# First MLP of a three-stage kernel: the next expert's first matrix is converted ahead of the ReLU, and the second MLP's weights are loaded two slots ahead

## The chip, the cores and the metric

The kernel runs on one core of one Trainium2 chip. The metric is the time of one execution on the device in microseconds (us), the median of several runs. Below, PE is TensorE, ACT is ScalarE, DVE is VectorE, POOL is GpSimd and SP is SyncE, which here only issues DMAs.

## The reference

A recurrent attention, then a mixture of eight experts with one expert for each token, then a plain gated MLP on all 3072 tokens. All in float32:

```python
def _moe_ref(x, modality_id, w_gate, modality_bias, w1, w2):   # x: (3072, 320), 8 experts, F = 1024
    logits = x @ w_gate + modality_bias[modality_id]
    e_idx = np.argmax(logits, axis=1)
    ...
    for e in range(E):
        mask = e_idx == e
        h = np.maximum(x[mask] @ w1[e], 0.0)
        out[mask] = gate_w[mask, None] * (h @ w2[e])

def _moe2_ref(x, w_in, w_out):                                  # w_in: (320, 2048), w_out: (2048, 320)
    h = x @ w_in
    g = h * (1.0 / (1.0 + np.exp(-1.702 * h)))
    return g @ w_out

def reference(**kwargs):
    ...
    return _moe2_ref(x=_moe_ref(x=attention, **moe), **moe2)
```

## The kernel before

Three stages follow each other on PE: the attention with the routing, the first MLP (the experts) and the second MLP. The change is in the first MLP, `moe1`, whose instructions stand in each engine's queue in the order in which they are written (`manual_schedule(engines=None)`): each engine takes its own queue strictly in that order, and semaphores hold an instruction until its operands are there.

Tokens are sorted by expert into slots of 128 rows. Slots 0 to 2 are done before this stage; `moe1` does slots 3 to 25 (`PLAN` is 3, `FIRST` is 4, `NFIX` is 26). Every float32 operand is carried as two float16 halves, high and low.

- `up` is a slot's 64 up products on PE: eight groups of eight, each into a quarter of a PSUM bank, five with the high half of the expert's first matrix and three with its low half. Then come the ReLU's halves: `hh` on ACT, twice 128x512, and `hl` = the rest on DVE, twice.
- `down` is the slot's 24 down products with the second matrix; ACT scales the sum into `ys`, POOL copies a token number into it, and SP stores it.
- `renew(i, n)` stands in an `If` on whether slot i has another expert than slot i-1. Where it has, `split(n)` converts the float32 matrix that lies ready in `raw1` or `raw2` into halves (ACT the high ones, DVE the low ones; eight pieces of 128x384 for the first matrix, five of 128x512 for the second), and POOL fetches the matrix that follows. All engines pass the branch, taken or not, and PE's low-half products wait until DVE has passed it. In this input the expert changes at slots 12, 14 and 25.
- `turn` transposes a slot's rows: on PE for slots 4 and 5, by a DMA transpose issued on SP three slots ahead for the others.
- `fill` is `step` of `weights2`. The second MLP's weights come as float64 in 22 parts of 512 KB (`s`). A step first writes the halves of the part before (ACT `WH` or `OH`, then DVE `WL` or `OL`), then issues the next part's load on SP, then makes float32 of its own part with five DVE instructions (`words`).
- `backs` and `flags` are small DVE work, once, after slot 8's `down`; `ready2` prepares the second MLP's first block in slots 16 to 23.
- `last` is the place for the second matrix of slot 25. It lies on the first matrix' halves, so it is written after slot 25's up products.

One iteration i of the loop is in this order: load of slot i+4's rows, `turn(i+3)`, `up(i+1)` with its ReLU halves, `renew(i+2, 1)`, `down(i)`, `renew(i+1, 2)`, `fill`. On PE up products of one slot and down products of the slot before alternate.

Of the kernel before, what the change touches and what calls it, by code (L numbers as in the profile page):

```python
# [484 lines left out]
F16 = mybir.dt.float16  # L485
# [22 lines left out]
PLAN = 3  # L508
# [3 lines left out]
class Mlp:  # L512
# [378 lines left out]
            out=xg.bitcast(I32), out_offset=None, in_=self.XD,  # L891
            in_offset=bass.IndirectOffsetOnAxis(ap=self.xrow[:, i:i + 1], axis=0))

    def up(self, xT, p, ps, mid=None, **k):

        nc = self.nc
        hh = p.tile([128, 8, 128], F16, tag="hh", name="hh")
        hl = p.tile([128, 8, 128], F16, tag="hl", name="hl")
        W = lambda t, k, f: t[:, f * 384 + k * 128:f * 384 + (k + 1) * 128]
        hi, lo = self.hi1, self.lo1  # L900
        for q in range(2):
            h = ps.tile([128, 4, 128], F32, tag="h", name="h", **k)
            for f4 in range(4):
                f = 4 * q + f4
                mms = [(W(hi, 0, f), xT[:, 0, :]), (W(hi, 1, f), xT[:, 1, :]), (W(hi, 0, f), xT[:, 2, :]),
                       (W(hi, 1, f), xT[:, 3, :]), (W(hi, 2, f), xT[:, 4, :]), (W(lo, 0, f), xT[:, 0, :]),
                       (W(lo, 1, f), xT[:, 1, :]), (W(lo, 2, f), xT[:, 4, :])]
                for j, (a, b) in enumerate(mms):
                    nc.tensor.matmul(h[:, f4, :], lhsT=a, rhs=b, start=(j == 0), stop=(j == 7))  # L909
            if mid and q == 0:  # L910
                mid()
            s = slice(4 * q, 4 * q + 4)
            nc.scalar.activation(hh[:, s, :], h, AF.Relu)  # L913
            nc.vector.scalar_tensor_tensor(hl[:, s, :], h, 0.0, hh[:, s, :], op0=ALU.max, op1=ALU.subtract)
        return hh, hl
# [35 lines left out]
    def moe1(self, fill, flags):  # L951
# [3 lines left out]
        with tc.tile_pool(name="m1", bufs=2, side="right", reuse_waits="tile") as p, \  # L955
# [16 lines left out]
            def turn(i):  # L972
                t = p.tile([128, 5, 128], F16, tag="xT", name="xT", bufs=3)
                x = xs[i].bitcast(F16)[:, 0:640]
                if i >= FIRST + 2:
                    nc.sync.dma_start_transpose(out=t, in_=x)
                else:
                    b = bank().bitcast(F16)[:, 0:640].rearrange("p (a b) -> p a b", a=5)
                    for j in range(5):
                        nc.tensor.transpose(b[:, j, :], x[:, 128 * j:128 * (j + 1)], self.id16)  # L980
                    nc.scalar.copy(t, b)
                xs[i] = xs[i], t
# [1 line left out]
            def bank():  # L984
                return ps.tile([128, 512], F32, tag="t", name="t")

            def up(i, mid=None):
                hs[i] = self.up(xs[i][1], p, ps, mid, bufs=4)

            def down(i, **k):  # L990
                self.down(i, xs.pop(i)[0], *hs.pop(i), p, ps, **k)

            last = self.hi1[:, 0:NW2], self.lo1[:, 0:NW2]
            xs[PLAN] = self.x0[PLAN], self.xT3
            for i in range(FIRST, FIRST + 3):
                load(i)
            load(FIRST + 3)
            self.fetch(1, self.wrow[:, FIRST:FIRST + 1])
            up(PLAN, lambda: turn(FIRST))
            self.fetch(2, self.wrow[:, FIRST:FIRST + 1])  # L1000
            for i in range(PLAN, NFIX - 1):
                if FIRST + 3 < i + 4 < NFIX:
                    load(i + 4)
                if i + 3 < NFIX:
                    turn(i + 3)
                up(i + 1, (lambda: turn(i + 2)) if i == PLAN else None)
                if i + 2 < FIRST + 2:
                    pass
                elif i + 2 < NFIX:
                    renew(i + 2, 1)  # L1010
                else:
                    with tc.If(new[i + 1] > 0):
                        self.split(2, last)
                    with tc.If(new[i + 1] < 1):  # L1014
                        nc.vector.tensor_copy(last[0], self.hi2)
                        nc.vector.tensor_copy(last[1], self.lo2)
                down(i)
                if FIRST + 2 <= i + 1 < NFIX - 1:
                    renew(i + 1, 2)
                fill(i)  # L1020
                if NFIX - 10 <= i <= NFIX - 3:
                    self.ready2(0, i - NFIX + 10, bank)
                if i == 8:
                    self.backs(bank()[:, 0:NE])
                    flags()
                if i == 14:
                    self.gather2(0)
                    nc.scalar.activation(self.between, self.between, AF.Sigmoid)
            down(NFIX - 1, to=last)
            fill(NFIX - 1)  # L1030

    def slots(self, fit, p, ps):

# [51 lines left out]
    def weights2(self, w_in, w_out, ctx):  # L1085
# [6 lines left out]
        n = 512  # L1092

        def load(src):
            s = q.tile([128, n], mybir.dt.uint64, tag="s", name="s")
            nc.sync.dma_start(out=s, in_=src)
            return s

# [16 lines left out]

        parts = [(w_in[:, k, a:a + n], lambda f, k=k, a=a: up(f, k, a)) for a in range(0, FF2, n) for k in range(3)]
        parts += [(flat(w_out)[:, n * i:n * i + n], lambda f, i=i: down(f, i)) for i in range(10)]
        staged, singles = [load(parts[0][0])], []

        def step():  # L1120

            if singles:
                f, work = singles.pop()
                work(f)
            if parts:
                work = parts.pop(0)[1]
                if parts:
                    staged.append(load(parts[0][0]))
                singles.append((single(staged.pop(0)), work))

        return step

    def before2(self, ctx):

# [787 lines left out]
def body(tc, A, out):  # L1922
    nc = tc.nc
    with ExitStack() as ctx:
# [8 lines left out]
        with ExitStack() as c1:  # L1933
# [53 lines left out]
            m.tab = ctx.enter_context(tc.tile_pool(name="tab", bufs=1, reuse_waits="tile"))  # L1987
            m.next(pool("m1x", 5))
            step = m.weights2(A["wi"], A["wo"], ctx)
            m.moe1(lambda i: step(), lambda: at.good(nc, m))  # L1990
        m.moe2(out)

        rv = nc.values_load(m.usual[0:1, 0:1], min_val=0, max_val=1)
# [36 lines left out]
```

## Time and profile before

| | |
|---|---|
| median of 3 runs | 1097.01 us (1094.71 to 1107.36) |
| the profiled execution | 1101.7 us, span of its instructions 1099.9 us |
| mean granted clock of TensorE | 0.883 of full speed |
| busy over the span | PE 914.2 us (83%), DVE 856.9 us (78%), ACT 676.5 us (62%), POOL 140.5 us (13%) |
| first MLP on PE | 563.6 to 760.2 us of the span |

The busy shares are means over three stages. For the first MLP the times from 563.6 to 760.2 us are to be read: what PE does there, how long it waits, and for whom. Times in the rows are microseconds from the start of the span.

### The profile page before, as it was taken

How to read it: one execution, taken by the hardware profiler on the slowest of the kernel's cores; microseconds unless marked ns; L12 is line 12 of the kernel's file. 1: busy time of each engine (PE TensorE's matmuls, PEld its weight loads, DVE VectorE, ACT ScalarE, POOL GpSimd, SP SyncE). 2: the span in 40 equal slices, each digit the busy share in tenths (PEclk: the TensorE clock that was granted, in tenths of full speed). 3: DMA queues.
4: the chain of work that ended last, by engine and by line, in shares of the span. 5: the costliest groups of instructions: out<-in, count | busy, mean ns of one | idle time of the engine just before them, and what ended most of it. 6: DMA issues, size and time to landing. Idle time of an engine off the chain costs nothing. (4 is left out here: it accounts for less than half of the span.)

```text
span 1099.9 us, 36916 instructions
## 1 busy us (share of the span) xinstructions
PE 914.2 (83%) x15548; PEld 672.5 (61%) x15548; DVE 856.9 (78%) x2094; ACT 676.5 (62%) x1476; POOL 140.5 (13%) x222
## 2 busy tenths in 40 slices
PE   0167886878798887889797888898999999999995
PEld 0155675666676666667686777784555555555553
DVE  8998999999999899988763887687666666666652
ACT  4477998998899899877632254243443434343432
POOL 2000000020020020011431223202012121111100
PEclk9999778987666786678799889998999999999998
DMA  3569779689869689695578668674011121121101
GB/s 112 128 151 182 142 157 176 115 179 187 174 159 179 135 169 185 106 133 91 186 145 148 147 184 237 156 150 126 7 31 42 31 43 34 41 35 43 37 1 27
DMA packets 249881, 129.53 MB, mean 118 GB/s; under 512 B 233248, under 2 KB 237088, under 8 KB 248544
## 3 DMA queue, kind: packets, MB, share of 16 engines
q1 hardware_dynamic: 243792, 98.34, 48.3%
q0 software_dynamic: 5808, 28.58, 8.5%
q8 instruction: 124, 2.03, 0.8%
q14 instruction: 61, 0.50, 0.1%
q10 hardware_dynamic: 96, 0.08, 0.0%
HBM read 57.78 MB, written 12.16 MB: 64 GB/s over the span
## 5 line engine op out<-in xcount | busy, mean ns | idle before, releaser
L1232 ACT ACTIVATE sg<-t 128x512 f32<-128x512 f32 x96 | 60.5, 630 | 183.7 <-DVE t L1230 183.7
L1226 PE MATMUL h<-xT,WH 128*128 128x512 f16 x480 | 119.3, 379 | 1.8 <-DVE g L1236 1.8
L1250 PE MATMUL acc<-OH,gh 128*128 128x320 f16 x384 | 114.8, 299 | 1.0 <-ACT gh L1238 1.0
L1250 PE MATMUL acc<-OH,gl 128*128 128x320 f16 x384 | 114.8, 299 | 0.6 <-DVE gl L1242 0.6
L1250 PE MATMUL acc<-OL,gh 128*128 128x320 f16 x384 | 114.8, 299 | 0.0
L909 PE MATMUL h<-xT,split 128*128 128x128 f16 x1408 | 91.9, 229 | 20.2 <-DVEq L964 11.5
L909 PEld LDWEIGHTS <-split 128*128 128x128 f16 x1472 | 91.7, 103 | 23.7 <-DVEq L964 12.9
L1230 DVE TENSOR_TENSOR t<-h,sB 128x512 f32<-128x512 f32 x96 | 66.2, 690 | 46.3 <-PE h L1226 46.3
L1250 PEld LDWEIGHTS <-gh 128*128 128x128 f16 x768 | 74.8, 98 | 44.3 <-ACT gh L1238 1.6
L1242 DVE TENSOR_TENSOR gl<-g,gh 128x512 f16<-128x512 f32 x96 | 66.3, 691 | 43.6 <-ACT gh L1238 43.6
L250 POOL DMA_INDIRECT XD<-XR,desti x24 | 31.1, 1295 | 468.0 <-ACT ust L250 314.9
L925 PE MATMUL y<-split,hh 128*128 128x320 f16 x368 | 81.2, 306 | 5.2 <-DVEq L1014 4.7
L1226 PE MATMUL h<-xT,WL 128*128 128x512 f16 x288 | 77.8, 379 | 0.0
L1226 PEld LDWEIGHTS <-WH 128*128 128x128 f16 x480 | 46.6, 98 | 44.8 <-DVE g L1236 3.4
L250 PE MATMUL w<-s,pick 128*128 128x160 f16 x368 | 65.5, 295 | 6.4 <-DVE s L250 2.3
L250 PEld LDWEIGHTS <-kb 64*128 64x128 f16 x2208 | 48.1, 101 | 35.6 <-issue 22.5
L1236 DVE SCALAR_TENSOR_TENSOR g<-h,sg 128x512 f32<-128x512 f32 x96 | 65.3, 680 | 0.0
L250 PEld LDWEIGHTS <-tbd 128*128 128x128 f16 x1152 | 51.2, 104 | 22.7 <-issue 9.9
L913 ACT ACTIVATE hh<-h 128x512 f16<-128x512 f32 x46 | 27.1, 594 | 54.2 <-PE h L909 54.1
L1238 ACT CAST gh<-g 128x512 f16<-128x512 f32 x96 | 59.3, 618 | 1.4 <-DVE g L1236 1.4
L925 PE MATMUL y<-split,hl 128*128 128x320 f16 x184 | 56.2, 306 | 0.0
L1264 POOL DMA_INDIRECT out<-o,ti x20 | 22.0, 1102 | 227.2 <-ACT o L1256 224.4
(357 smaller groups left out, 2403.4 us busy)
## 6 DMA issues: line engine op xcount, KB each, us to landing
K<-in_KVR SPq DMA_DIRECT2D x24, 480.0 KB, 4.9
raw<-in_AB SPq DMA_DIRECT2D x13, 640.0 KB, 4.0
s<-in_wi SPq DMA_DIRECT2D x12, 512.0 KB, 8.7
s<-in_wo SPq DMA_DIRECT2D x10, 512.0 KB, 4.8
raw<-in_WU SPq DMA_DIRECT2D x6, 660.0 KB, 4.2
YS<-ys SPq DMA_DIRECT2D x23, 160.5 KB, 6.4
Sd<-s SPq DMA_TRANSPOSE x46, 3.5
out<-o SPq DMA_DIRECT2D x14, 40.0 KB, 3.2
```

Of the source, the lines that this page charges most:

```text
L250: r = self.made[i] = getattr(getattr(self.nc, e), op)(*a, **k)
L909: nc.tensor.matmul(h[:, f4, :], lhsT=a, rhs=b, start=(j == 0), stop=(j == 7))
L913: nc.scalar.activation(hh[:, s, :], h, AF.Relu)
L925: nc.tensor.matmul(y, lhsT=a[:, f, :], rhs=V(b, f), start=(n == 0), stop=(n == 23))
L1226: nc.tensor.matmul(h3, lhsT=a, rhs=r, start=(j == 0), stop=(j == 7))
L1230: nc.vector.tensor_tensor(t, hs[k], self.xs[steps[k][0]]["sB"], op=ALU.mult)
L1232: nc.scalar.activation(sgs[k], t, AF.Sigmoid, scale=1.702)
L1236: nc.vector.scalar_tensor_tensor(gs[k], hs.pop(k), 2.0 ** -4, sgs.pop(k), op0=ALU.mult, op1=ALU.mult)
L1238: nc.scalar.copy(ghs[k], gs[k])
L1242: nc.vector.tensor_tensor(gls[k], gs.pop(k), ghs[k], op=ALU.subtract)
L1250: nc.tensor.matmul(accs[c], lhsT=a[:, s], rhs=r[:, f, :], start=(f == 0 and j == 0), stop=(f == NF - 1 and j == 2))
L1264: sent.append(nc.gpsimd.indirect_dma_start(out=out, out_offset=bass.IndirectOffsetOnAxis(ap=X["ti"][:, c:c + 1], axis=0), in_=o, in_offset ...
```

## The change

`up` is parted into `products` (PE alone) and `relu` (the halves), and `step` into `convert` (the halves of the part before) and `gather` (load and `words`). An iteration is now: `turn(i+3)`, the up products of slot i+1, `convert`, `renew(i+2, 1)`, the ReLU halves of slot i+1, `down(i)`, `renew(i+1, 2)`, `gather`. Two parts of `s` are loaded before the loop, and each `gather` loads the part two further on, into three buffers. `turn` is on PE for slots 4 to 7. `last` is a tile of its own, and slot 25's second matrix is converted into it ahead of slot 25's up products. `flags` comes two slots later.

```diff
-    def up(self, xT, p, ps, mid=None, **k):
-
-        nc = self.nc
-        hh = p.tile([128, 8, 128], F16, tag="hh", name="hh")
-        hl = p.tile([128, 8, 128], F16, tag="hl", name="hl")
+    def up(self, xT, p, ps):
+        return self.relu(self.products(xT, ps), p)
+
+    def products(self, xT, ps, mid=None, **k):
+
+        nc = self.nc
+        hs = []
...
+            hs.append(h)
             if mid and q == 0:
                 mid()
+        return hs
+
+    def relu(self, hs, p):
+
+        nc = self.nc
+        hh = p.tile([128, 8, 128], F16, tag="hh", name="hh")
+        hl = p.tile([128, 8, 128], F16, tag="hl", name="hl")
+        for q, h in enumerate(hs):
             s = slice(4 * q, 4 * q + 4)
             nc.scalar.activation(hh[:, s, :], h, AF.Relu)
...
-                if i >= FIRST + 2:
+                if i >= FIRST + 4:
                     nc.sync.dma_start_transpose(out=t, in_=x)
...
-            last = self.hi1[:, 0:NW2], self.lo1[:, 0:NW2]
+            last = p.tile([128, 2, NW2], F16, tag="last", name="last", bufs=1)
+            last = last[:, 0], last[:, 1]
...
-                if i + 3 < NFIX:
+                if FIRST + 4 <= i + 3 < NFIX:
                     turn(i + 3)
-                up(i + 1, (lambda: turn(i + 2)) if i == PLAN else None)
-                if i + 2 < FIRST + 2:
-                    pass
-                elif i + 2 < NFIX:
-                    renew(i + 2, 1)
-                else:
+                if i + 2 == NFIX:
                     with tc.If(new[i + 1] > 0):
                         self.split(2, last)
                     with tc.If(new[i + 1] < 1):
                         nc.vector.tensor_copy(last[0], self.hi2)
                         nc.vector.tensor_copy(last[1], self.lo2)
+                h = up(i + 1)
+                fill[0]()
+                if FIRST + 2 <= i + 2 < NFIX:
+                    renew(i + 2, 1)
+                hs[i + 1] = self.relu(h, p)
                 down(i)
                 if FIRST + 2 <= i + 1 < NFIX - 1:
                     renew(i + 1, 2)
-                fill(i)
+                fill[1]()
...
                 if i == 8:
                     self.backs(bank()[:, 0:NE])
+                if i == 10:
                     flags()
...
-            s = q.tile([128, n], mybir.dt.uint64, tag="s", name="s")
+            s = q.tile([128, n], mybir.dt.uint64, tag="s", name="s", bufs=3)
...
-        staged, singles = [load(parts[0][0])], []
+        staged, singles = [load(parts[i][0]) for i in range(2)], []
...
-                if parts:
-                    staged.append(load(parts[0][0]))
+                if len(parts) > 1:
+                    staged.append(load(parts[1][0]))
```

One iteration in DVE's queue, before. `split_152` is the first matrix, `split_153` the second, the `wt` row is the first of the five of `words`; rows marked BRANCH are the `If`:

```order
L914 SCALAR_TENSOR_TENSOR hl<-h,hh 128x512 x2
L963 TENSOR_LOAD chg
L964 COMPARE_AND_BRANCH
L886 SCALAR_TENSOR_TENSOR split_152<-raw_150,split_152 128x384 x8
L964 UNCONDITIONAL_BRANCH x2
L964 COMPARE_AND_BRANCH
L886 SCALAR_TENSOR_TENSOR split_153<-raw_151,split_153 128x512 x5
L964 UNCONDITIONAL_BRANCH x2
L1106 SCALAR_TENSOR_TENSOR WL<-f,WH 128x512
L1079 TENSOR_SCALAR wt<-s 128x512
```

The same iteration in DVE's queue, now:

```order
L1120 SCALAR_TENSOR_TENSOR WL<-f,WH 128x512
L974 TENSOR_LOAD chg
L975 COMPARE_AND_BRANCH
L886 SCALAR_TENSOR_TENSOR split_152<-raw_150,split_152 128x384 x8
L975 UNCONDITIONAL_BRANCH x2
L925 SCALAR_TENSOR_TENSOR hl<-h,hh 128x512 x2
L975 COMPARE_AND_BRANCH
L886 SCALAR_TENSOR_TENSOR split_153<-raw_151,split_153 128x512 x5
L975 UNCONDITIONAL_BRANCH x2
L1093 TENSOR_SCALAR wt<-s 128x512
```

The first matrix and its branch now stand ahead of `hl`, and `words` directly behind the second matrix; the next row behind the five of `words` is `WL` of the same part, where before it was `hl`.

SP's queue at the start of the stage, before (`xT` rows are DMA transposes, of slots 6 and 7):

```order
L1096 DMA s<-in_wi 128x512
L250 DMA YS<-xg_154 128x321
L976 DMA_TRANSPOSE xT<-xg 128x5x128
L934 DMA YS<-ys 128x321
L1096 DMA s<-in_wi 128x512
L976 DMA_TRANSPOSE xT<-xg 128x5x128
```

SP's queue at the start of the stage, now:

```order
L1110 DMA s<-in_wi 128x512 x2
L250 DMA YS<-xg_154 128x321
L945 DMA YS<-ys 128x321
L1110 DMA s<-in_wi 128x512
L974 TENSOR_LOAD chg
L974 ISA x2
L975 COMPARE_AND_BRANCH
L975 UNCONDITIONAL_BRANCH x2
L945 DMA YS<-ys 128x321
L1110 DMA s<-in_wi 128x512
L987 DMA_TRANSPOSE xT<-xg 128x5x128
```

Two parts are asked for at once, and the first DMA transpose, now slot 8's, comes behind the fourth part.

DVE's queue at the end of the stage (iteration 24), before:

```order
L914 SCALAR_TENSOR_TENSOR hl<-h,hh 128x512 x2
L1012 COMPARE_AND_BRANCH
L886 SCALAR_TENSOR_TENSOR split_152<-raw_151,split_152 128x512 x5
L1012 UNCONDITIONAL_BRANCH x2
L1014 COMPARE_AND_BRANCH
L1015 COPY split_152<-split_153 128x2560
L1016 COPY split_152<-split_153 128x2560
L1014 UNCONDITIONAL_BRANCH x2
L1106 SCALAR_TENSOR_TENSOR OL<-f,OH 128x512
```

DVE's queue at the end of the stage, now:

```order
L1020 COMPARE_AND_BRANCH
L886 SCALAR_TENSOR_TENSOR last<-raw_151,last 128x512 x5
L1020 UNCONDITIONAL_BRANCH x2
L1022 COMPARE_AND_BRANCH
L1023 COPY last<-split_153 128x2560
L1024 COPY last<-split_153 128x2560
L1022 UNCONDITIONAL_BRANCH x2
L1120 SCALAR_TENSOR_TENSOR OL<-f,OH 128x512
L925 SCALAR_TENSOR_TENSOR hl<-h,hh 128x512 x2
```

Slot 25's `hl` is now the last of this chain, behind the second matrix and a part's `OL`.

## Rows read from the trace of the kernel before

**Rows 1.** Windows view, first and second MLP: busy us and count of each engine, granted clock.

```profile
563.60:760.20 196.60, 171.19 (x2042) 145.84 (x2040) 135.51 (x255) 74.81 (x142) 42.94 (x59) 0.93 0.76 175
760.20:1099.90 339.70, 325.06 (x1942) 188.22 (x1939) 209.98 (x369) 140.36 (x263) 43.02 (x64) 0.99 0.13 31
```

**Rows 2.** Waits of PE's matmuls in the first MLP: us in total, times, longest.

```profile
PE h L909 <- DVEq L964: 11.5, 5, 4.1
PE h L909 <- DMA xT<-xg: 4.9, 1, 4.9
PE y L925 <- DVEq L1014: 4.7, 1, 4.7
PE h L909 <- DVE split L886: 3.5, 1, 3.5
```

**Rows 3.** PE's timeline: start, duration, operation, count, in brackets the wait before.

```profile
586.43 5.05 PE L909 MATMUL h<-xT,split 128*128 128x128 f16 x64 [4.86 <-DMA xT<-xg]
...
596.73 3.47 PE L909 MATMUL h<-xT,split 128*128 128x128 f16 x59 [1.71 <-DVEq L964]
...
603.30 3.74 PE L909 MATMUL h<-xT,split 128*128 128x128 f16 x64
606.87 0.30 PE L925 MATMUL y<-split,hh 128*128 128x320 f16 x1
...
610.13 3.74 PE L909 MATMUL h<-xT,split 128*128 128x128 f16 x64
...
628.34 5.96 PE L909 MATMUL h<-xT,split 128*128 128x128 f16 x59 [4.07 <-DVEq L964]
...
674.84 4.94 PE L909 MATMUL h<-xT,split 128*128 128x128 f16 x59 [2.90 <-DVEq L964]
...
699.54 3.47 PE L909 MATMUL h<-xT,split 128*128 128x128 f16 x59 [2.55 <-DVEq L964]
...
734.43 3.74 PE L909 MATMUL h<-xT,split 128*128 128x128 f16 x64
...
754.09 0.43 PE L925 MATMUL y<-split,hh 128*128 128x320 f16 x1 [4.70 <-DVEq L1014]
```

**Rows 4.** Windows view of two stretches behind a wait (clock is third from the end).

```profile
628.30:634.10 5.80, 5.76 (x59) 5.76 (x60) 4.13 (x7) 0.60 (x1) 0.00 (x0) 0.54 0.69 148
...
754.10:760.20 6.10, 6.10 (x25) 3.50 (x26) 3.56 (x6) 0.00 (x0) 2.02 (x2) 0.53 0.87 164
```

**Rows 5.** Windows view at the stage's start: last two columns are DMA share, GB/s.

```profile
569.00:572.00 3.00, 3.00 (x51) 2.81 (x49) 0.69 (x1) 1.68 (x3) 1.25 (x3) 1.00 1.15 353
572.00:584.00 12.00, 9.57 (x109) 7.68 (x106) 5.61 (x9) 2.88 (x6) 1.10 (x1) 1.00 1.08 88
```

**Rows 6.** DMA view, slot 8's rows, issued at 569.22: us to landing.

```profile
xg<-XD,xrow POOLq DMA_INDIRECT x1, 21.2
```

**Rows 7.** DVE's timeline, columns as in Rows 3.

```profile
592.35 0.43 DVE L1079 TENSOR_SCALAR wt<-s 128x512 int32<-128x512 int32 x1 [8.98 <-DMA s<-in_wi]
...
595.34 1.28 DVE L914 SCALAR_TENSOR_TENSOR hl<-h,hh 128x512 f16<-128x512 f32 x2
597.07 0.69 DVE L1106 SCALAR_TENSOR_TENSOR WL<-f,WH 128x512 f16<-128x512 f32 x1 [0.45 <-DVEq L964]
...
600.66 1.28 DVE L914 SCALAR_TENSOR_TENSOR hl<-h,hh 128x512 f16<-128x512 f32 x2
...
622.34 0.21 DVE L820 TENSOR_TENSOR rnm<-rot,t 128x64 f32<-128x64 f32 x1
...
625.61 0.15 DVE L1887 TENSOR_REDUCE all<-n 128x1 f32<-128x8 f32 x1
...
626.95 1.28 DVE L914 SCALAR_TENSOR_TENSOR hl<-h,hh 128x512 f16<-128x512 f32 x2
...
635.74 3.84 DVE L886 SCALAR_TENSOR_TENSOR split<-raw,split 128x384 f16<-128x384 f32 x8
...
645.63 3.10 DVE L886 SCALAR_TENSOR_TENSOR split<-raw,split 128x512 f16<-128x512 f32 x5 [1.03 <-ACT split L885]
```

**Rows 8.** Groups view, the first MLP, ACT: busy us, mean ns of one, idle before.

```profile
L1105 ACT ACTIVATE WH<-f 128x512 f16<-128x512 f32 x12 | 7.5, 626 | 3.0 <-DVE f L1083 2.2
```

More of the change, by code (lines that the diff above doesn't have):

```diff
@@ L985, in bank, with up @@
                 return ps.tile([128, 512], F32, tag="t", name="t")
-            def up(i, mid=None):
-                hs[i] = self.up(xs[i][1], p, ps, mid, bufs=4)
+            def up(i):
+                j = i + 1
+                return self.products(xs[i][1], ps, (lambda: turn(j)) if j < FIRST + 4 else None, bufs=4)
             def down(i, **k):
                 self.down(i, xs.pop(i)[0], *hs.pop(i), p, ps, **k)
-            last = self.hi1[:, 0:NW2], self.lo1[:, 0:NW2]
+            last = p.tile([128, 2, NW2], F16, tag="last", name="last", bufs=1)
+            last = last[:, 0], last[:, 1]
             xs[PLAN] = self.x0[PLAN], self.xT3
@@ L998, in moe1 @@
             self.fetch(1, self.wrow[:, FIRST:FIRST + 1])
-            up(PLAN, lambda: turn(FIRST))
+            hs[PLAN] = self.relu(up(PLAN), p)
             self.fetch(2, self.wrow[:, FIRST:FIRST + 1])
@@ L1028, in moe1 @@
                     nc.scalar.activation(self.between, self.between, AF.Sigmoid)
+            fill[0]()
             down(NFIX - 1, to=last)
-            fill(NFIX - 1)
     def slots(self, fit, p, ps):
@@ L1117, in weights2, with convert @@
         parts += [(flat(w_out)[:, n * i:n * i + n], lambda f, i=i: down(f, i)) for i in range(10)]
-        staged, singles = [load(parts[0][0])], []
-        def step():
+        staged, singles = [load(parts[i][0]) for i in range(2)], []
+        def convert():
             if singles:
@@ L1124, in step, with gather @@
                 work(f)
+        def gather():
             if parts:
                 work = parts.pop(0)[1]
-                if parts:
-                    staged.append(load(parts[0][0]))
+                if len(parts) > 1:
+                    staged.append(load(parts[1][0]))
                 singles.append((single(staged.pop(0)), work))
-        return step
+        return convert, gather
     def before2(self, ctx):
@@ L1989, in body @@
             step = m.weights2(A["wi"], A["wo"], ctx)
-            m.moe1(lambda i: step(), lambda: at.good(nc, m))
+            m.moe1(step, lambda: at.good(nc, m))
         m.moe2(out)
```

## The prediction

> **What bounds the kernel now.** I read the windows of the stages first. The second MLP is 339.7 us with PE busy for 325.06 at a clock of 0.99: the change leaves it alone, and it starts when the first MLP's last down products are done, so a microsecond saved in the first MLP is one saved in the kernel. The first MLP takes 196.6 us [rows 1]. A slot without trouble takes PE 6.83 us: its up products start at 603.30, the down products at 606.87, the next up products at 610.13, so 3.57 and 3.26 [rows 3]. Twenty-three slots are 157 us. Some 39 us of the stage are therefore loss.
>
> The waits view says where 24.6 of them go: 11.5 us in five waits of the low-half products for DVE to pass a branch, 3.5 us in one wait for a piece of the first matrix, 4.9 us for one DMA transpose, 4.7 us for the branch before `last` [rows 2]. PE's timeline gives the places: 4.86 at slot 6, 1.71 at slot 7, 4.07 at slot 11, 2.90 at slot 16, 2.55 at slot 19, 4.70 before the last down products [rows 3]; the 3.5 falls at slot 14 and the fifth branch wait, 0.28, later.
>
> Most of the rest is the clock. Behind the wait of 4.07 us 59 products take 5.96 us, against 3.47 for 59 behind the waits of 1.71 and of 2.55; behind 2.90 they take 4.94 [rows 3]. Behind the 4.07 the granted clock is 0.54, and 0.53 in the last down products, which take 6.1 us instead of 3.26 [rows 3, 4]: near the lower of TensorE's two levels, 1.2 of 2.4 GHz. So a wait of up to 2.55 us cost only itself here, and one of 2.90 or more 1.3 to 2.8 us besides.
>
> **The change part by part.** *Start.* Slot 6 now turns on PE. The wait of 4.86 and the slow products behind it (5.05 instead of 3.74) go; two turns more on PE cost five products each, 0.28 us at the pitch of 3.57 over 64. Gain 4.86 + 1.31 - 0.56 = 5.6 us. Slot 7's wait came from `words`: DVE sat 8.98 us until 592.35 for the second part [rows 7], and the branch that PE wants stands behind it. That part is now asked for at the start: gain 1.7 us.
>
> What is late next there is the third part, issued where the second was, and slot 8's rows, which landed 21.2 us after their issue, at 590.4 [rows 6]. PE wants slot 8 at 603.30 - 4.86 - 1.31 - 1.71 + 0.56 = 596.0. Through 569 to 572 the DMAs moved 353 GB/s, then 88 for 12 us [rows 5], while two DMA transposes and the fetches of both matrices were under way. I take it that the transposes held the rest up, since the burst without them (2.9 MB of matrices, 1.5 MB of parts, at 353 GB/s) is 13 us long, and count nothing for slot 8; if they didn't, it is a rival below.
>
> The rows only show that it landed late. The Trainium skill (DMA: Bandwidth & Descriptors, Queues, rings and completion order) says that a DMA's completion lands only after every earlier write of the same DMA engine, whichever queue it came from. By that rule the third part waits for the matrices as the second did, and the time is the first rival's.
>
> *Middle, slots 11 to 16.* Two expert changes, `backs` and `flags` fall here, and DVE is the bound. Its time for a plain slot is 5.32 us, from one pair of `hl` to the next (595.34 to 600.66: `hl` 1.28, branch 0.45, `WL` 0.60, `words` 2.99) [rows 7]. In the new order `WL` stands directly behind `words`, and ACT's `WH` lies between them: 0.63 us [rows 8] and 0.07 of passing on, so 0.70 in which DVE idles whenever it is behind. That is a wait that the change adds; queued behind it are the branch for PE and the ReLU halves. Now the sum, from the up products of slot 9 at P. Their `hl` end at P + 5.0 (3.57, some 0.15 to ACT, `hh` 0.6, `hl` 0.7), `words` at P + 8.0. From there to the branch that slot 16's low-half products want, DVE does `backs` 3.27 and `flags` 1.34, five slots of 5.32, two first matrices of 3.84, two second ones of 3.10 [rows 7], four gaps of 0.70 (two of six are filled by `backs` and `flags`), and a last `WL` and branch, 1.1: 49.0 us, so P + 57.0. PE without a wait would be there at P + 7 x 6.83 + 0.28 = P + 48.1. PE is late by 8.9 us. It is paid in pieces, slot by slot, of 1 to 2.5 us, and I count no lower clock for them, as behind 1.71 and 2.55. ACT does no more than before, and reaches a first matrix earlier; the fetch for it is issued as much earlier.
>
> Before, this stretch paid 4.07 + 3.54 + 2.90 = 10.5 us of waits, and 2.5, 2.5 and 1.5 us of slow products (5.96 - 3.47, the same again at slot 14, 4.94 - 3.47): 17.0. Gain 17.0 - 8.9 = 8.1 us.
>
> *Slots 19 and 21.* The 2.55 us stood behind a part that landed late; two slots ahead its load has 13.7 us. The wait and the 0.28 go: 2.8 us.
>
> *End.* Before, from slot 24's up products at 734.43 to the last down products at 754.09 there were 19.66 us [rows 3]. Now, from slot 24's up products at P: `ys`, `WH` and `WL` let DVE go at about P + 2.4, then come the first matrix with its branch 4.3, `hl` 1.28, `words` 2.99, `ready2`'s halves 0.7, `last` 3.10 with its branches 0.3, `OL` 0.60, `hl` 1.28: P + 16.9. PE is there at P + 13.9, so it waits 3.0 us instead of 4.70. That is 2.8 us less on the way. The lower clock behind it cost 6.1 - 3.26 = 2.8; behind 3.0 I take 2.0, between 1.5 (after 2.90) and 2.5 (after 3.54 and 4.07). Gain 3.6 us.
>
> Sum: 5.6 + 1.7 + 8.1 + 2.8 + 3.6 = 21.8 us. The profiled execution would go from 1101.7 to 1079.9; the median of the runs lies 4.7 us below it, so I take the sum off that: 1097.0 - 21.8 = **1075.2 us**, 2.0% faster, just where a measurement of this kernel begins to tell a change from none.
>
> **Rivals.** *The start isn't eased.* The third part lands at 592.35 again: `words` 2.99, the gap 0.70, `WL` and branch 1.1 end at 597.2, and PE wants the branch at 596.3. DVE then enters the middle about 2 us late, of which a plain slot (5.32 + 0.70 of 6.83) gives back 0.8. Together 3 us: 1078. The 21.2 us of slot 8's rows speak for it, the 88 GB/s against.
>
> *The waits of the middle only change places.* DVE is the bound there in both orders, and the gap of 0.70 is new. If the new waits come in one piece and lower the clock as before, the stretch costs its 17 us again: 1075.2 + 8.1 = 1083; with the end unchanged too, 1087. For it: 49.0 us of DVE work against 40.1 of PE. Against it: the branch now comes before `hl`.
>
> *DVE is less late than reckoned.* The gap is hidden, ACT runs ahead, and half of the 8.9 and the 3.0 with its clock go: 1068.
>
> *The lower clock stays.* If many short waits in slots 12 to 16 bring PE down to its lower level and it doesn't rise, a slot costs 6.5 (64 products at 5.96 for 59) + 6.1 = 12.6 instead of 6.83. The gain is gone when four slots beyond the middle run so, and with all nine of slots 17 to 25 the kernel is slower: 1075 + 52 = 1127. Against it: the clock was full again in every slot after the long waits, e.g. 603.30 and 734.43 [rows 3]. The Trainium skill (TensorE: Matmul & The Clock Gate, What's actually happening) says that the lower level is the default and that activity releases it; by that a PE that waits in every slot could stay there, though no row here shows a slot that did.
>
> **How the numbers follow.** Forecast (1071 to 1078) 0.42, start not eased 0.20, waits change places 0.18, DVE less late 0.16, lower clock stays 0.04. The range leaves out the last and the outer ends of the second and third: 1066 to 1087. Faster by over 2% means under 1075.1: half of the forecast, the less-late case and a little of the first rival, 0.44; slower 0.04; the rest 0.52.
>
> **What would show it.** No wait of PE for a DMA transpose and none of DVE for `s` before slot 8; no wait at slot 19; in slots 12 to 16 several waits of 1 to 2.5 us that add up to some 9, at a clock near 1; ACT's `WH` waiting for `words` there; one wait of about 3 us before the last down products; the second MLP starting near 738. I'd be wrong most easily if the DMA burst at the start takes another form, or if `hl` or `WH` in the middle bind earlier than the branch.

## The result, and the profile of the kernel after

The kernel after takes 1082.06 us (median of 4 runs, 1077.33 to 1087.37) beside 1099.3 for the kernel before (4 runs, 1094.71 to 1107.36): ratio 0.9847, 95% interval 0.9803 to 0.9891. That is 16.8 us less, between 12.0 and 21.7, and the whole interval lies below 1, but by the bound of 2%, under which two kernels count as the same, the two are the same. The forecast was 21.8 us less. The time lies inside the range, 7 us above the forecast.

The profiled execution has a span of 1080.2 us. The windows view of its first and second MLP (us, busy time and count of PE, PEld, DVE, ACT, POOL, granted clock, DMA share, GB/s) answers to [rows 1]:

```profile
569.70:740.80 171.10, 162.17 (x2052) 138.73 (x2050) 137.35 (x255) 75.28 (x144) 37.84 (x58) 0.99 0.77 196
740.80:1080.20 339.40, 325.07 (x1942) 188.21 (x1939) 210.38 (x370) 140.35 (x263) 44.39 (x66) 0.99 0.13 32
```

The first MLP is 25.5 us shorter than in the profile of before, at a clock of 0.99 instead of 0.93, and the second as long. But it begins at 569.7 instead of 563.6: the stage before ended 6.1 us later, although its instructions are the same in the same order on every engine. So the span fell by 19.7. Whether the 6.1 us belong to the change is asked of the chip below.

The waits of PE's matmuls in the first MLP (us in total, times, longest), against [rows 2]:

```profile
PE h L911 <- ACTq L975: 2.7, 3, 1.6
PE h L911 <- ACT split L885: 1.9, 1, 1.9
PE h L911 <- DVEq L975: 1.5, 3, 0.8
PE y L936 <- DVEq L1022: 1.1, 1, 1.1
PE y L936 <- DVE hl L925: 1.1, 1, 1.1
PE h L911 <- DVE split L886: 0.4, 1, 0.4
```

There are 8.7 us where there were 24.6, and the profile names no DMA among them. PE's timeline gives the places (start, duration, operation, count, in brackets the wait before), against [rows 3]:

```profile
601.75 3.74 PE L911 MATMUL h<-xT,split 128*128 128x128 f16 x64
608.58 3.74 PE L911 MATMUL h<-xT,split 128*128 128x128 f16 x64
...
637.69 3.47 PE L911 MATMUL h<-xT,split 128*128 128x128 f16 x59 [0.83 <-DVEq L975]
646.34 0.45 PE L911 MATMUL h<-xT,split 128*128 128x128 f16 x5 [1.93 <-ACT split L885]
647.18 5.12 PE L911 MATMUL h<-xT,split 128*128 128x128 f16 x59 [0.39 <-DVE split L886]
...
664.67 0.45 PE L911 MATMUL h<-xT,split 128*128 128x128 f16 x5 [1.56 <-ACTq L975]
665.64 3.47 PE L911 MATMUL h<-xT,split 128*128 128x128 f16 x59 [0.51 <-DVEq L975]
...
721.07 3.74 PE L911 MATMUL h<-xT,split 128*128 128x128 f16 x64
...
736.26 0.30 PE L936 MATMUL y<-last,hh 128*128 128x320 f16 x1 [1.14 <-DVEq L1022]
737.65 0.31 PE L936 MATMUL y<-last,hl 128*128 128x320 f16 x1 [1.09 <-DVE hl L925]
```

Slots 3 to 11 run without a wait (slot 8 starts at 601.75, 32.0 us after the first up products instead of 39.7). Slots 13 to 16 pay in pieces, slot 19 a little (0.87 us; the profile names ACT's branch, but slot 19's DMA transpose landed at 686.77 and PE went on at 686.91), and two waits stand before and in the last down products. From slot 9's up products at 608.58 to the low-half products of slot 16 at 665.64 are 57.06 us; the prediction had reckoned DVE's chain to that point as 57.0.

To set kernels beside each other I use PE's timeline alone: the time from a slot's first up product to a later slot's, and from slot 25's to the second MLP's first. A slot without trouble takes 6.83, so slots 8 to 16 take 61.5, 17 to 21 34.2, 22 to 24 20.7 as they are coded. Each row is one profiled execution:

| kernel | stage before ends | 3 to 7 | 8 to 16 | 17 to 21 | 22 to 24 | 25 | first MLP | second MLP |
|---|---|---|---|---|---|---|---|---|
| before | 563.6 | 39.7 | 79.6 | 37.6 | 21.0 | 18.7 | 196.6 | 339.7 |
| after | 569.7 | 32.0 | 70.5 | 35.2 | 20.7 | 12.7 | 171.1 | 339.4 |
| before_again | 586.0 | 31.5 | 79.4 | 37.2 | 21.0 | 17.2 | 186.2 | 339.8 |
| after_again | 586.6 | 32.0 | 72.1 | 34.6 | 20.7 | 12.7 | 172.1 | 339.9 |
| e1_turns_alone | 562.7 | 32.0 | 78.3 | 40.1 | 21.0 | 17.4 | 188.9 | 338.9 |
| e2_loads_alone | 563.2 | 32.8 | 75.1 | 40.0 | 21.0 | 18.3 | 187.1 | 339.7 |
| e3_order_alone | 564.5 | 32.2 | 73.2 | 40.5 | 20.7 | 16.5 | 183.2 | 338.9 |
| e4_last_undone | 566.4 | 32.0 | 70.6 | 35.6 | 20.7 | 15.1 | 174.1 | 340.0 |
| e5_backs_early | 585.0 | 32.1 | 68.9 | 35.2 | 20.7 | 14.4 | 171.2 | 340.3 |
| e6_branch_first | 580.7 | 32.0 | 68.5 | 37.9 | 20.7 | 12.9 | 172.1 | 340.6 |
| e7_tail | 581.6 | 32.0 | 72.0 | 35.1 | 20.7 | 13.3 | 173.2 | 340.0 |
| e9_defer | 581.7 | 32.0 | 65.0 | 41.5 | 20.7 | 12.7 | 171.9 | 346.9 |
| e10_all | 558.3 | 32.1 | 65.3 | 34.7 | 20.7 | 14.4 | 167.2 | 340.9 |
| e11_nodefer | 561.1 | 32.1 | 69.2 | 34.7 | 20.7 | 13.1 | 169.8 | 338.4 |

Kernels sent together share a chip and the runs of before: e1 to e4; before_again, after_again, e5 and e6; e7 and e9; e10 and e11. Before took 1098.0, 1110.0, 1108.8 and 1094.7 us on these four, so only ratios are set beside each other across them. Four of the 25 runs of before on the chip of e1 to e4 are slow, over 1.5% above the fastest, and are left out of the ratios; the other 21 take 1086.0 to 1101.5.

### The profile page after: what moved, and what is told of

Read it like the earlier page. It is cut to its first block, busy times and chain, and to the rows that moved or that the text cites. A ratio compares the mean times of both kernels' runs of the same rounds, so it can differ in the third digit from the quotient of the medians.

```text
span 1080.2 us, 36938 instructions
## 1 busy us (share of the span) xinstructions
PE 902.3 (84%) x15558; PEld 664.0 (61%) x15558; DVE 858.6 (79%) x2094; ACT 676.5 (63%) x1478; POOL 135.3 (13%) x222
## 5 line engine op out<-in xcount | busy, mean ns | idle before, releaser
L911 PEld LDWEIGHTS <-split 128*128 128x128 f16 x1472 | 85.3, 99 | 10.2 <-ACTq L975 4.2
L911 PE MATMUL h<-xT,split 128*128 128x128 f16 x1408 | 85.1, 221 | 6.7 <-ACTq L975 2.7
L936 PE MATMUL y<-split,hh 128*128 128x320 f16 x352 | 75.3, 299 | 0.0
L1251 DVE SCALAR_TENSOR_TENSOR g<-h,sg 128x512 f32<-128x512 f32 x96 | 65.3, 680 | 0.0
L936 PE MATMUL y<-split,hl 128*128 128x320 f16 x176 | 52.6, 299 | 0.0
L1241 PEld LDWEIGHTS <-WL 128*128 128x128 f16 x288 | 28.2, 98 | 34.0
```

The source lines that it names most:

```text
L936: nc.tensor.matmul(y, lhsT=a[:, f, :], rhs=V(b, f), start=(n == 0), stop=(n == 23))
L1241: nc.tensor.matmul(h3, lhsT=a, rhs=r, start=(j == 0), stop=(j == 7))
L1251: nc.vector.scalar_tensor_tensor(gs[k], hs.pop(k), 2.0 ** -4, sgs.pop(k), op0=ALU.mult, op1=ALU.mult)
```

## The experiments

My theory on the result: the four parts of the change add up, the start, the middle, slots 19 and 21 and the end each giving about what the table's rows of before and after show. Rivals: one part carries the others, or a loss of before belonged to one execution.

**Both kernels again.** Nothing is edited.

> The kernel before, unchanged, profiled once more. Asked of it: whether the 7.7 us that slots 3 to 7 lost in its profiled execution (39.7 us instead of 32.0) belong to the kernel or to that execution, since two kernels that still turn slots 6 and 7 by DMA lost only 0.2 and 0.7 us there; and how far the end of the stage before (563.6 us) moves between executions. Theory that the loss belongs to the kernel's order: slots 3 to 7 take 39 to 41 us again. Rival (the burst takes one form or another from execution to execution): 32 to 35 us. The middle, which is set by DVE, takes 78 to 80 us in either case.

> The kernel after, unchanged, for a second profile and a closer interval. Theory (the 6.1 us by which the stage before ended later in the profile of after belong to that execution, since its instructions are the same on every engine): that stage ends anywhere from 562 to 570 us, the first MLP takes 171 us again within 1, and the ratio to before falls to 0.977 to 0.985. Rival (the change makes the stage before longer): it ends at 569 to 570 again and the ratio stays at 0.985 or above.

Before ran in 1107.7 us beside 1110.0 (ratio 0.9982, interval 0.9956 to 1.0007), after in 1098.8 (0.9878, 0.9840 to 0.9915: 13.5 us less, 9.4 to 17.8). In before_again slots 3 to 7 take 31.5 us: the wait of 4.86 us for a DMA transpose, the slow products behind it and the 1.71 us of slot 7 aren't there. The rival holds; the middle takes 79.4, as expected of either case. The windows of its start (columns as above):

```profile
586.00:595.00 9.00, 9.00 (x150) 8.62 (x148) 1.95 (x3) 4.00 (x7) 2.52 (x5) 1.00 1.03 274
595.00:598.00 3.00, 3.00 (x34) 2.43 (x33) 2.87 (x6) 0.53 (x1) 0.00 (x0) 1.00 1.13 87
```

The slow stretch, 88 GB/s for 12 us in [rows 5], is there with 87 GB/s, but for 3 us, too short to reach PE. Nor is the lower clock always there: behind slot 14's wait of 3.54 us in the profile of before 59 products took 5.99 us at a clock of 0.55, behind nearly the same wait here they take 3.62 at 1.00 (PE's timeline of before, then of before_again):

```profile
655.58 5.99 PE L909 MATMUL h<-xT,split 128*128 128x128 f16 x59 [3.54 <-DVE split L886]
```

```profile
669.57 3.62 PE L909 MATMUL h<-xT,split 128*128 128x128 f16 x59 [3.47 <-DVE split L886]
```

Of the stage before: it ends at 586.0 in the one and 586.6 in the other, and between 580.7 and 586.6 for the four kernels on that chip. The rival that the change lengthens it falls; 6 us are what executions differ by. The theory's own numbers for after_again were missed as well: 562 to 570 us for that end, which on this chip lies 17 to 24 us later in both kernels, and a ratio of 0.977 to 0.985, which came out at 0.9878. The two profiles differ by 14.1 us in the first MLP, and the runs by 13.5.

**The turns alone.** Before, with `if i >= FIRST + 4` for the DMA turn and the PE turns of slots 6 and 7 in the up products of slots 5 and 6:

```
-                if i >= FIRST + 2:
+                if i >= FIRST + 4:
...
-                up(i + 1, (lambda: turn(i + 2)) if i == PLAN else None)
+                up(i + 1, (lambda: turn(i + 2)) if i + 2 < FIRST + 4 else None)
```

> The kernel before, with slots 6 and 7 turned on PE as the only change; parts are still asked for one slot ahead. The measure is the first MLP, from its first up products to the second MLP's first ones: 196.6 us before, 171.1 after. Theory of the prediction (the DMA transposes held up the rest of the burst): slot 6's wait of 4.9 us goes, the second part lands well before 592.35 - 563.61 = 28.7 us after the first up products, so slot 7's wait of 1.7 us goes as well; slots 3 to 7 take 33 to 34 us instead of 39.7 and the first MLP some 190. Rival (the burst is bound by its bytes or its order of completion): the second part lands at the same 28 to 29 us; then PE, 5.6 us earlier, waits 6 to 7 us for the branch behind words in slot 7, slots 3 to 7 take 39 to 40 and the first MLP stays at 195 to 197.

1091.45 us, ratio 0.9931 (0.9896 to 0.9965). Slots 3 to 7 take 32.0, a little less than the theory's 33 to 34, and PE doesn't wait in slot 7; the rival falls. Slots 17 to 21 take 40.1: at slot 19 PE waits 3.57 us behind a part that landed late, where before waited 2.55 and before_again 1.03. The rest is as before. By times the turns gain 7.6 us on average there (3.8 to 11.4); in the profiles they take away a loss of 8.2 us where it comes (39.7 against 31.5), and cost some 0.55 where it doesn't (32.0 against 31.5). How often the loss comes is not settled: of four profiles with DMA turns of slots 6 and 7 one has it, while 7.6 us on average is what it would give if it came in every execution of before on that chip.

**The loads alone.** Before, with three tiles `s`, two parts asked for at the start and each later one two slots ahead, as in the change.

> The kernel before, with parts asked for two slots ahead as the only change; slots 6 and 7 are still turned by DMA. Theory: the wait of 1.7 us in slot 7 goes and so do the 2.55 us in slot 19 and the 0.28 us in slot 21, since each part has 13.7 us; slot 6 still waits 4.9 us for its DMA transpose; first MLP 196.6 - 4.5 = 192. Rival (the extra part lengthens the burst, whose DMA time is what slot 6 waits for): slot 6 waits 6 to 8 us and the gain of the early part is gone; first MLP 194 to 197, with only slot 19's wait missing.

1090.84 us, ratio 0.9954 (0.9909 to 1.0000). First MLP 187.1, below both forecasts, because slots 3 to 7 take 32.8. The slow stretch is there all the same, in windows of e2 and, in the last row, of e3, which turns slots 6 and 7 by DMA too:

```profile
575.20:578.20 3.00, 3.00 (x53) 2.89 (x51) 0.89 (x2) 0.86 (x2) 0.00 (x0) 1.00 1.28 171
578.20:581.20 3.00, 2.96 (x22) 1.91 (x20) 0.69 (x1) 0.34 (x1) 0.00 (x0) 1.00 1.18 37
573.50:576.50 3.00, 3.00 (x35) 2.43 (x34) 2.18 (x5) 0.53 (x1) 0.00 (x0) 1.00 0.07 28
```

The second matrix landed 13.7 us after its issue in e2 and 14.7 in e3, against 22.0 in before and, with slots 6 and 7 on PE, 9.1 in e1 and 10.7 in after. Slot 6's transpose took 17.4 us in e2, and PE waited 1.15. So all four profiles with these turns show a slow stretch; PE wants slot 6's rows some 16.5 us after their transpose is issued, and only in that of before do they come much later. Two more readings are new. Slots 8 to 16 take 75.1 instead of 79.4 to 79.6: there `words` had waited 2.0 us (before) and 3.6 (before_again) for parts that landed late, and in e2 it waits for none. And slots 17 to 21 are not better but 40.0: the wait at slot 19 is still there, 3.92 us, now for a DMA transpose. The theory's 2.55 us at slot 19 fall; see slot 19 below.

**The order alone.** After, with turns, loads, `last` and flags set back.

> The kernel after, with only its order of DVE and ACT left: the part's halves and the branch for the first matrix ahead of the ReLU's halves, the words behind the down products. Slots 6 and 7 are turned by DMA, parts come one slot ahead, the last second matrix is made in the first one's place behind the last up products, the flags stand in slot 9 as before. Theory: slots 3 to 7 cost 39 to 40 us as before, slots 8 to 16 some 70.5 us instead of 79.6 (the flags in the same stretch as before, so nothing from them), slot 19's wait for a late part stays; of the 6.0 us by which slot 25 came out shorter, 1 to 2 come with the order; first MLP 185 to 188. Rival (the middle is eased because the start is: DVE enters it with its backlog gone): slots 8 to 16 keep 77 to 80 us and the first MLP 194 or more.

1092.24 us, ratio 0.9951 (0.9920 to 0.9981). Slots 8 to 16 take 73.2, 6.2 us less than in before_again, whose start is as free of the loss (32.2 and 31.5); the rival falls. The theory had 70.5 there and 39 to 40 for the start, so the first MLP, 183.2, is below its 185 to 188. The loads alone gave 4.2 to 4.4 in this stretch and the order 6.2, both together with the flags moved 7.3 to 9.1 in the two profiles of after: they overlap in part. Slot 19 waits 4.0 us, slot 25 takes 16.5.

**`last` set back.** After, with `last` in the first matrix's place, behind the last up products and ReLU halves:

```
-            last = p.tile([128, 2, NW2], F16, tag="last", name="last", bufs=1)
-            last = last[:, 0], last[:, 1]
+            last = self.hi1[:, 0:NW2], self.lo1[:, 0:NW2]
...
                 hs[i + 1] = self.relu(h, p)
+                if i + 2 == NFIX:
...
```

> The kernel after, with the last second matrix made in the first one's place, behind the last up products and their ReLU halves, as before. Everything up to slot 24 is as after. Theory of the prediction's term for the end: PE waits some 4.7 us before the last down products, and they run at the lower clock: slot 25 takes 18 to 19 us as before instead of 12.7, first MLP 177. Rival (the end was eased by words and the ReLU halves standing otherwise, whichever tile the matrix goes to): slot 25 takes 13 to 15 us, first MLP 171 to 173.5.

1079.90 us, ratio 0.9814 (0.9750 to 0.9879). Slot 25 takes 15.1, just above the rival's 13 to 15 and far from the theory's 18 to 19: one wait of 3.27 us instead of 2.2 in two, and a granted clock of 0.66 behind it. That is 2.5 us more than in after, but only 0.8 more than in e5 and e10, which have the new `last` and took 14.4 at a lower clock. So of the 4.5 to 6.0 us by which slot 25 got shorter, 0.8 to 2.5 belong to `last`; how the order, the loads and the clock share the rest is not shown (e3, with the order alone, took 16.5). The time itself can't tell 2.5 us.

**`backs` and flags early.** After, with `backs` at loop index 4 and `flags` at 5 instead of 8 and 10.

> The kernel after, with backs moved from slot 9 to slot 5 and the flags from slot 11 to slot 6, where DVE has idle time; nothing else. Theory (DVE's work bounds slots 8 to 16): 4.6 us of DVE work leave that stretch and two gaps of 0.70 come back, which backs and flags had filled; the stretch loses 5 to 6 us instead of 9.0, so it takes 66.5 to 67.5 us instead of 70.5, and the first MLP 167 to 168. Rival (what bounds it is the chain from a first matrix's landing over ACT's and DVE's halves to PE, not the sum of DVE's work): slots 8 to 16 take 69.5 to 70.5 us. Second rival: slots 3 to 7 grow from 32.0 by 2 us or more, as backs delay the branches there.

1095.69 us, ratio 0.9842 (0.9796 to 0.9888). Slots 8 to 16 take 68.9, between theory and first rival; the first MLP, 171.2, misses the theory's 167 to 168, in part because slot 25 took longer. From slot 9's up products to slot 16's low halves are 55.53 us instead of 57.08, so of the 3.2 us that were to leave the chain 1.5 did. From slot 14 on PE's waits are those of after_again to 0.1 us. On the way DVE itself now waits, 1.0 us for ACT's halves of slot 12's second matrix (DVE's timeline of e5), where in after it didn't wait:

```profile
652.63 3.10 DVE L886 SCALAR_TENSOR_TENSOR split<-raw,split 128x512 f16<-128x512 f32 x5 [1.01 <-ACT split L885]
```

So work ahead of that place is part of DVE's chain only as far as DVE is late there. Slot 25 took 14.4 with the same two waits as after, 1.15 and 1.10 us: behind them the clock was 0.64 here and 1.00 in after (windows of the last down products of e5, then of after):

```profile
751.40:756.20 4.80, 4.78 (x23) 2.94 (x24) 3.97 (x7) 0.63 (x1) 2.47 (x4) 0.64 0.69 109
```

```profile
737.60:740.80 3.20, 3.15 (x24) 2.28 (x25) 3.06 (x6) 0.00 (x0) 1.48 (x3) 1.00 0.67 110
```

**The branch first.** After, with `renew(i + 2, 1)` ahead of `fill[0]()`.

> The kernel after, with the part's halves (WH, WL) behind the branch and the first matrix's halves instead of ahead of them, still ahead of the ReLU's halves. Theory (the gap of 0.70 us behind words and ACT's wait for words are costs of the new order): ACT makes a first matrix while DVE is in words, PE gets its branch some 1.3 us earlier, and in slots with a new first matrix the gap is covered by its halves; slots 8 to 16 take 67.5 to 69.5 us instead of 70.5. Rival (DVE's sum of work bounds the stretch and the gap only moves in front of WL): 70 to 71 us. Second rival: WH now stands behind the first matrix on ACT and the ReLU's halves later, so the down products wait, and the stretch takes 71.5 us or more.

1096.53 us, ratio 0.9875 (0.9826 to 0.9924). Slots 8 to 16 take 68.5, within the theory's numbers, but the next five 37.9 instead of 34.6 to 35.2: slot 17 lost 3.8, in two waits of 0.48 and 1.08 us that the profile puts down to nothing and a clock of 0.76. Together 106.4 us beside 106.7 of after_again. Whether the loss in slot 17 belongs to the edit can't be told from one profile.

**The last two parts later.** After, with `fill[1]()` left out at loop indices 23 and 24 and done, with its halves, behind the last down products.

> The kernel after, with the words and halves of the last two parts moved behind the last down products; nothing else. In the kernel after, the words of the last part but one (2.99 us) stand on DVE ahead of the halves of the last second matrix, and that part's OL ahead of the last ReLU halves, and PE waits 1.14 + 1.09 us for these. Theory: both waits go, slot 25 takes 10.4 to 10.9 us instead of 12.7, the second MLP keeps 339 to 340 us, since the two parts are wanted there only some 45 us after its start. Rival (the work only changes places): DVE comes to the second MLP's first gates about 4 us later, PE waits for them there, and the second MLP takes 341 to 344 us.

1098.67 us, ratio 0.9893 (0.9832 to 0.9954). Both waits of slot 25 go and the second MLP takes 340.0, as in the theory, but slot 25 takes 13.3 instead of 10.4 to 10.9: PE waits instead for the last DMA transpose of the second MLP's rows (PE's timeline, the second MLP's first products):

```profile
754.77 1.25 PE L1244 MATMUL h<-xT,WH 128*128 128x512 f16 x5 [3.06 <-DMA xT<-x]
```

It was issued at 743.61, 11 us earlier. Neither theory nor rival had this: the next bound was a transfer.

**Three parts out of the middle.** After, with `fill[1]()` left out at loop indices 11 to 13, and the three parts done in whole in steps 1 to 8 of the second MLP.

> The kernel after, with no words (and in the slot after, no halves of a part) in slots 12 to 14, where two expert changes fall; the three parts that are then left over are done in steps 1 to 8 of the second MLP. Theory (the sum of DVE's work bounds slots 12 to 16): three times words 2.99, gap 0.70 and WL 0.69 leave the chain, 13 us, against the 9 to 10.6 us that PE loses in slots 8 to 16; the stretch takes 61.5 to 64.5 us instead of 70.5 to 72, the first MLP 163 to 165, and the second MLP 339 to 341 (DVE is busy there for 62% of the time). Rival (the path is the first matrix: its fetch, ACT's halves, PE's wait for the first of them): slots 8 to 16 take 67 us or more. Second rival: the second MLP pays it back, 344 us or more.

1101.93 us, ratio 0.9918 (0.9888 to 0.9948). The waits of PE in the first MLP, then in the second one's first 77 us:

```profile
PE h L911 <- DMA xT<-xg: 6.5, 2, 4.6
PE y L936 <- DVEq L1022: 1.1, 1, 1.1
...
PE h L911 <- DVEq L975: 0.8, 1, 0.8
...
```

```profile
PE acc L1266 <- DVE gl L1258: 4.2, 6, 1.3
PE h L1242 <- DVE g L1252: 1.6, 1, 1.6
PE h L1200 <- DVE g L1252: 1.1, 1, 1.1
```

The main theory holds in its place: slots 8 to 16 take 65.0, at the edge of the 61.5 to 64.5 expected, and of that 1.85 is a wait for a transpose; no wait for a matrix's halves is left, so the sum of DVE's work bounds the middle, not the matrix's fetch. But PE, 6 us earlier, runs into two DMA transposes, 1.85 and 4.64 us, so that the first MLP takes 171.9 instead of 163 to 165, and the second MLP is 7 us longer, as the second rival said: DVE comes late with `gl` and `g` behind each run of `words`.

**What the runs point to.** After, with `backs` and flags early as in e5; the gather of the second MLP's first rows at loop index 15 instead of 14; slots 17 to 19 turned on PE; and in e10 alone no `words` at indices 12 and 13, the two parts done in the second MLP one instruction in each step, behind `g`, where DVE waits 0.69 us for ACT:

```
+            onPE = lambda i: i < FIRST + 4 or 17 <= i <= 19
...
-                fill[1]()
+                if i not in (12, 13):
+                    fill[1]()
...
-                if i == 14:
+                if i == 15:
                     self.gather2(0)
...
                     high(k - 1)
+                next(rest, None)
```

> The kernel after, with what the runs so far point to: backs and flags in slots 5 and 6; no words in slots 13 and 14, the two parts left over done in the second MLP one instruction at a time, each in the 0.69 us in which DVE waits there for ACT; the gather of the second MLP's first rows one slot later, behind the token of slot 15; slots 17 to 19 turned on PE. Theory (DVE's sum bounds slots 12 to 16, and behind it come the DMA transposes that stand behind the gather and beside a matrix's fetch): slots 8 to 16 take 65 to 67.5 us instead of 70.5 to 72, slots 17 to 21 take 35 to 35.5 with the three turns, slot 25 takes 12.7 to 14.4; first MLP 166 to 168 instead of 171 to 172; second MLP 339 to 341, where three parts in whole pieces cost it 7 us. Ratio to before 0.980 to 0.985. Rival (an instruction more in each of DVE's gaps delays the low halves there as well): the second MLP takes 343 us or more and the kernel is no faster than after.

> The same without the deferral: the kernel after with backs and flags in slots 5 and 6, the gather one slot later, slots 17 to 19 turned on PE; all 22 parts stay in the first MLP. Theory: slots 8 to 16 take 68.5 to 69.5 us as with backs and flags moved alone, slots 17 to 21 take 35 to 35.5, first MLP 169 to 170, second MLP 339 to 340; 2 to 3 us more than with the deferral. Rival (the waits at slots 18 and 19 came from DVE and not from the gather): slots 17 to 21 take 36 us or more, as PE pays for three turns and gets nothing.

e10 takes 1068.88 us, ratio 0.9762 (0.9735 to 0.9789); e11 1072.78, ratio 0.9810 (0.9765 to 0.9855). The windows of e10's two MLPs:

```profile
558.30:725.40 167.10, 162.15 (x2066) 138.88 (x2064) 131.03 (x244) 76.48 (x146) 39.06 (x59) 0.99 0.74 198
725.40:1066.30 340.90, 325.12 (x1942) 188.21 (x1939) 215.32 (x381) 140.83 (x264) 43.25 (x64) 0.99 0.13 32
```

The stretches came out as in the theories: 65.3 and 69.2 us for slots 8 to 16, 34.7 for 17 to 21 with the turns, 340.9 for e10's second MLP. e10's ratio lies below the 0.980 to 0.985 expected. e10 is faster than before by more than 2%, and its interval lies below both of after's. After itself wasn't run on that chip, and by the profiles e10's two MLPs are only 2.5 to 4.0 us shorter than after's, so how much of the distance to after is e10's own stays open. So does what the deferral is worth: the theory had 2 to 3 us, but by the profiles e10's first MLP is 2.7 us shorter than e11's and its second 2.5 longer (340.9 against 338.4), together 0.2; the runs differ by 3.9, their intervals overlap, and in the two profiles the stage before makes up most of the difference (558.3 and 561.1).

## Why the prediction was right, and where it was off

The range held and the mechanism it put most on, DVE's chain through slots 11 to 16, was the one at work. The forecast of 21.8 us lies between the two pairs of profiles, 25.5 and 14.1, and just above the measured 12.0 to 21.7. By its steps:

*Start, 7.3 us forecast.* 7.7 by the first pair of profiles, -0.5 by the second. The burst was read rightly: in after 371 GB/s in the 3 us at the rows' place in [rows 5] and 228 behind them, no transpose beside it, the second matrix in 10.7 us instead of 22.0. The rival of a late third part is out, as it landed 4.9 us after its issue:

```profile
575.00:578.00 3.00, 3.00 (x52) 2.85 (x50) 0.79 (x2) 1.56 (x3) 1.35 (x3) 1.00 1.00 371
578.00:590.00 12.00, 12.00 (x154) 10.33 (x153) 8.34 (x14) 3.58 (x7) 0.71 (x1) 1.00 0.63 228
```

What was off is that the term was taken whole from one execution: "The wait of 4.86 and the slow products behind it go" supposes that they are always there. They were in one profile of four, though a slow stretch was in all four. This accounts for all of the distance between the forecast of 21.8 us and the 14.1 of the second pair. The times don't settle how often the loss comes: the 7.6 us of e1 fit one in nearly every execution on that chip, the 13.5 us of after_again fit none on its chip.

The Trainium skill (Advanced Engine Details and Errata, X-Bar Transpose (TRN2)) says that transpose DMAs are as fast as regular ones, 350 to 400 GB/s expected. The two stretches at 87 and 88 GB/s here lie far below that, but they mix DMA transposes with indirect fetches; no run here measured the rate of a transpose by itself, so the page's figure is not tested.

*Middle, 8.1 us forecast.* 9.1 and 7.3 (79.6 to 70.5, 79.4 to 72.1). From slot 9's up products to slot 16's low halves there were 57.06 and 57.08 us for the 57.0 of DVE's chain. Part of the gain is probably the loads', which the term did not count: with the order alone the stretch keeps 73.2 (e3), and the loads alone shorten it by 4.2 to 4.4 (e2). The gap of 0.70 us behind `words` is there, in the rows of DVE's timeline:

```profile
645.69 0.69 DVE L1120 SCALAR_TENSOR_TENSOR WL<-f,WH 128x512 f16<-128x512 f32 x1 [0.70 <-ACT WH L1119]
...
655.51 0.69 DVE L1120 SCALAR_TENSOR_TENSOR WL<-f,WH 128x512 f16<-128x512 f32 x1 [0.70 <-ACT WH L1119]
```

and ACT waits 24.6 us in ten slots for `words` before `WH`, as said. Two inputs were off without moving the sum, so that it came out to 0.1 us is partly luck. `backs` and flags count for about half of what the sum gave them (e5). And "I count no lower clock" didn't hold: behind 1.93 and 0.39 us in slot 14 59 products took 5.12 instead of 3.47, 1.65 us more. In after_again the same two waits cost almost nothing besides, and slot 16 paid instead (PE's timeline):

```profile
664.02 3.62 PE L911 MATMUL h<-xT,split 128*128 128x128 f16 x59 [0.37 <-DVE split L886]
...
682.56 5.05 PE L911 MATMUL h<-xT,split 128*128 128x128 f16 x59 [0.51 <-DVEq L975]
```

So the rule that the prediction read from one profile, that a wait of up to 2.55 us costs only itself and one of 2.90 or more 1.3 to 2.8 us besides, doesn't hold from execution to execution; behind 3.47 us in before_again 0.15 us was lost. In after, seven waits make 5.7 us of the 9.0 lost, not all of it.

*Slots 19 and 21, 2.8 us forecast.* 2.4 and 2.5, so the number was right, with the wrong cause. The wait of 2.55 us did stand behind a late part, but the part was late because it was issued late, at 689.63 in before, where SP had issued nothing since 679.7. The same hold makes the next transpose late, and in after 0.87 us remain; with the loads alone (e2) 3.92. POOL's and SP's timelines of after show the chain:

```profile
670.37 0.97 POOL L1161 DMA_INDIRECT xg<-YS,back  x1 [6.42 <-DVE f L1097]
...
677.39 0.27 POOL L1167 CAST ti<-xg 128x4 int32<-128x4 f32 x1 [2.25 <-DMA xg<-YS,back]
...
680.13 0.36 POOL L939 COPY ys<-xg 128x1 f32<-128x1 f32 x1 [0.64 <-DMA xg<-XD,xrow]
```

```profile
668.55 1.24 SPq L987 DMA_TRANSPOSE xT<-xg  x1
680.52 0.34 SPq L945 DMA_DIRECT2D YS<-ys  x1
681.14 0.33 SPq L1110 DMA_DIRECT2D s<-in_wo  x1
681.58 1.23 SPq L987 DMA_TRANSPOSE xT<-xg  x1
```

POOL does four gathers and two small operations that wait for them; the token of the next finished slot is queued behind, on SP the write of `YS` waits for the token, and the part and the next transpose stand behind the write. SP issues nothing for nearly 11 us. The prediction passed SP's and POOL's queues by here. With the gather one slot later and the turns on PE the stretch takes 34.7 in e10, where e9, whose PE comes as early, had 41.5; in e11 it takes 34.7 too, where after had 34.6 to 35.2, so there little or nothing is gained. The two edits were not tried apart.

*End, 3.6 us forecast.* 6.0 and 4.6. The chain was sized rightly: DVE ends the last `hl` at 738.19, 17.1 us after slot 24's up products, for 16.9. But PE doesn't wait for its end: it starts the down products on `last` at 736.26 and waits for `hl` inside them, 1.14 + 1.09 = 2.2 us instead of 3.0, and the clock stayed at 1.00, where 2.0 us had been put down. In e5 and e10 it did fall behind the same waits, and slot 25 took 14.4: the term is 3 to 6 us by execution.

Of the rivals, the lower clock that stays didn't come: the stage ran at 0.99, and in the middle one slot's clock fell, slot 14's in after (0.82) and slot 16's in after_again (0.81). The Trainium skill (TensorE: Matmul & The Clock Gate, What's actually happening) makes activity release the higher level; in after a PE that waited in four slots in a row, 13 to 16, and was busy for 7.3 of 9.0 us in slot 15, had a clock of 1.00 there, so nothing here disagrees.

## What to carry to other kernels

A stall that one profile shows beside a burst of DMAs should be priced with the chance that it is there: profile the kernel before more than once. Work out the busiest engine's chain from the instruction that frees its input, then look at what the faster engine meets next; here PE, 6 us earlier out of the middle in e9, ran into transposes that stood behind POOL's gather and SP's write. Work put off to another stage costs nothing only if each piece fits into a gap there: three parts in whole cost the second MLP 7 us, two parts by single instructions 1 to 2.5, about as much as they had saved.

## What the hardware showed that I had not expected

The same instructions of the stage before take 558 to 587 us from chip to chip, and up to 6 us more or less on one chip. A DMA transpose took 4.5 us to land at the start of after, but 17.4 for slot 6 in e2, and in before PE waited for the one issued at 564.98 until 586.43, both beside the fetches of the matrices. And two waits of 1.1 us left the granted clock at 1.00 in one execution and at 0.64 on average, so in part at the lower of TensorE's two levels of 1.2 and 2.4 GHz, in another.
